# An explicit per-engine order for the first stage of an attention and two-MLP kernel, with block pairs merged to 512 columns

## The chip, the cores and the metric

The kernel runs on one core of a Trainium2 chip. The metric is the device time of one execution in microseconds (us); lower is better. TensorE is called PE, VectorE DVE, ScalarE ACT, GpSimd POOL, SyncE SP in the views. SP computes nothing here: it issues the DMA transfers, in the order of its queue.

## What is computed

Attention with a window of 64 positions over 4 batches of 576 positions and 8 heads of 64, then two gated MLPs, all on 2304 tokens:

```python
scores = scale * np.matmul(q, k.transpose(0, 1, 3, 2))
mask = (rel >= 0) & (rel < window)            # window = 64
scores = np.where(mask, scores, -1000000000.0)
...
attn = attn / (np.sum(attn, axis=-1, keepdims=True) + 1e-09)
x = np.matmul(attn, v)                        # to 2304 x 512
...
gate = 1.0 / (1.0 + np.exp(-(x @ w_gate)))    # 512 x 1536
x = gate * (x @ w_val) @ w_out                # 1536 x 512
...
return (x @ w_a) * (x @ w_b) @ w_out
```

q, k, v and x are float32; the weights come as 8-byte words that the kernel turns into float32 itself.

## The kernel before

**Blocks and tiles.** The 2304 tokens are nine blocks of 256 columns, each of two attention tiles of 128 tokens: 18 tiles. Blocks 0 to 4 (tiles 1 to 10, counted from 1 here and from 0 in the names) are the front; blocks 5 to 8 are the back, whose attention runs as filler beside the MLPs of the front.

**An attention tile** (`attention`, L103 to L197): load k, q and v; transpose k and q on PE into PSUM (kps, qps, L118); copy them out to kt and qt (L125, L126) and bring the last 64 columns of the tile before into kt (L123; a tile that starts a sequence is zeroed there, L121); 32 score products (sps, L138); add the mask and take the row's extreme on DVE (L148); exponentials on ACT, each with a read of its running sum (L153); add a constant to the sums and take the reciprocal on DVE (L169, L170); scale on POOL (L171); transpose back (tps, L178) and copy out to pt (L179); products with v (xps, L186), for which parts of v are moved between partitions by DMA (vb, L161 and L165); and split the result into a high part on ACT (xh, L192) and a low part on DVE (xl, L193).

**Weights.** A weight number F has three matrices a, b and o of 512 KB. `load_weights` loads them; `decode` (L274 to L307) turns each into a high and a low part: two operations on ACT (low and ex, L282, L285), two on DVE (wi, L287, L290), one on POOL (L293), then DVE (ex, L295), ACT (L300) and DVE (L301). It saves the pair (ka, kb, ko, 512 KB each, L303) and, for a and b, the float32 matrix (kf, 256 KB, L305) to DRAM for later. There are two buffers for ex, one for low and wi, three for raw words, four for each decoded matrix.

**Units.** One unit is one block (256 columns) or pair of blocks (512 columns) with one weight number: 12 products for the gate (gps), 12 for the value (vps, L317), then tanh on ACT, a product on DVE (hr, L341), and a split into hh (ACT, L326) and hl (DVE, L327). After the units of a turn follow the down projections (accm, L405; four pieces for a pair, two for a block), held back until the next turn, each evacuated to gacc by a copy on ACT for the first turn of a block and by an addition on DVE (L385) after that.

**Order.** `FIRST` lists the turns of the front's first stage. Before, these are block 0 with weights 0 and 1; block 1 with 0 to 2; block 0 with 2; then blocks 2, 3 and 4 with 0 to 2 each: 15 units of 256 columns. Behind it the turns go by the groups (0), (1, 2), (3, 4); the first is block 0 with weight 3. Within this the program gives a work list, and a scheduler of the framework chooses for each engine the order in which the instructions stand, by its own estimate of when each could run:

```python
    FIRST = (
        ((("attention", 0), ("weights", 0), ("weights", 1), ("attention", 1)), 0, (0, 1)),
        ((("weights", 2), ("attention", 2)), 1, (0, 1, 2)),
        ((), 0, (2,)),
        ((("attention", 3),), 2, (0, 1, 2)),
        ((("attention", 4),), 3, (0, 1, 2)),
        ((), 4, (0, 1, 2)),
    )
```

Of the kernel before, what the change touches and what calls it, by code (L numbers as in the profile page):

```python
# [9 lines left out]
F32 = mybir.dt.float32  # L10
# [10 lines left out]
def tile_window_attention_gated_mlps(ctx, tc, q, k, v, w1g, w1v, w1o, w2a, w2b, w2o, out):  # L21
# [4 lines left out]
    P = 128  # L26
# [37 lines left out]

    mask_n = qp.tile([P, P], F32, name="mask_n")
# [36 lines left out]

    def attention(t, dst, c0):  # L103
# [3 lines left out]
        mask = edge_mask(starts[0]) if starts else mask_n  # L107
        raw = [load_tile(nm, src, t, work, "kq", 3) for nm, src in (("k", k), ("q", q))]
        v_own = load_tile("v", v, t, vs, "v", 3)
        yield  # L110

# [3 lines left out]
        kqps = [kp.tile([P, NP, P], F32, tag=kq_tag, name=f"{nm}ps{t}") for nm in "kq"]  # L115
        for ps, r in zip(kqps, raw):
            for j in range(NP):
                nc.tensor.transpose(ps[:, j, :], r[:, 2 * j:2 * j + 2, :], ident)  # L118
        kt = kts.tile([P, NP, KW], F32, tag="kt", name=f"kt{t}")
        if starts == [0]:  # L120
            nc.vector.memset(kt[:, :, before], 0.0)  # L121
        else:
            nc.gpsimd.tensor_copy(kt[:, :, before], prev["k"][:, :, last])  # L123
        qt = qp.tile([P, NP, P], F32, tag="qt", bufs=2, name=f"qt{t}")
        nc.scalar.activation(out=kt[:, :, own], in_=kqps[0], func=AF.Copy)  # L125
        nc.scalar.activation(out=qt, in_=kqps[1], func=AF.Copy, scale=QSCALE)  # L126
        prev["k"] = kt
        yield
# [13 lines left out]
        yield  # L142
        stat = small.tile([P, 3, 2, NP], F32, tag="stat", name=f"stat{t}")
        ssum, nmax, den = (stat[:, i] for i in range(3))
        pr = [work.tile([P, NP, P], F32, tag="pr", bufs=4, name=f"pr{t}_{e}") for e in range(2)]
        for e in range(2):
            for j in range(NP):
# [3 lines left out]
                )  # L151
            for j in range(NP):
# [4 lines left out]
            yield  # L157
# [6 lines left out]
        else:  # L164
            nc.sync.dma_start(out=v_before[lo], in_=prev["v"][hi])  # L165
        prev["v"] = v_own
        pt = [work.tile([P, NP, P], F32, tag="pt", bufs=2, name=f"pt{t}_{e}") for e in range(2)]
        for e in range(2):
            nc.vector.tensor_scalar(out=den[:, e], in0=ssum[:, e], scalar1=1.0e-9, scalar2=None, op0=ALU.add)  # L169
            nc.vector.reciprocal(out=den[:, e], in_=den[:, e])  # L170
            nc.gpsimd.tensor_tensor(  # L171
                out=pr[e], in0=pr[e], in1=den[:, e].unsqueeze(2).to_broadcast([P, NP, P]), op=ALU.mult
            )
            yield
        for e in range(2):
# [3 lines left out]
            nc.scalar.activation(out=pt[e], in_=tps, func=AF.Copy)  # L179
            yield  # L180
        xps = ps_at.tile([P, NP, P], F32, tag="at", name=f"xps{t}")
        for j in range(NP):
            for s, vv in enumerate((v_before, v_own)):
                rows = slice(s * WIN, (s + 1) * WIN)
                for e, dims in enumerate((lo, hi)):
                    nc.tensor.matmul(  # L186
                        xps[dims, j, rows], lhsT=vv[:, 2 * j + e, :], rhs=pt[e][:, j, rows], start=True, stop=True
                    )
        cols = slice(c0, c0 + P)
        if isinstance(dst, tuple):  # L190
            xhi, xlo = (d[:, :, cols] for d in dst)
            nc.scalar.activation(out=xhi, in_=xps, func=AF.Copy)  # L192
            nc.vector.tensor_tensor(out=xlo, in0=xps, in1=xhi.bitcast(F32), op=ALU.subtract)  # L193
# [3 lines left out]
        yield  # L197
# [35 lines left out]
    def attention_stream(blocks):  # L233
# [3 lines left out]
        for tick in range(1 << 30):  # L237
# [4 lines left out]
            for blk, u in list(live):  # L242
                if next(u, u) is u:
# [6 lines left out]

    mats = ((w1g, w1v, w1o), (w2a, w2b, w2o))
    words = [[w.bitcast(I32) for w in m] for m in mats]
    staged, ready = {}, {}
# [6 lines left out]
    def load_weights(F):  # L260
        ph, fc = divmod(F, NF)
        sl = slice(2 * fc * P, 2 * (fc + 1) * P)
        for nm, w in zip("abo", words[ph]):
            r = stage.tile([P, DM, 2], I32, tag="st", name=f"st_{nm}")
            if nm == "o":
                nc.sync.dma_start(out=r.rearrange("p f t -> p (f t)"), in_=w[fc * P:(fc + 1) * P, :])
            else:
                nc.sync.dma_start(
                    out=r.rearrange("p (c f) t -> p c (f t)", c=NP),
                    in_=w[:, sl].rearrange("(c p) f -> p c f", p=P),  # L270
                )
# [534 lines left out]
```

## Time and profile before

| | |
|---|---|
| median of 3 runs | 987.81 us (986.78 to 989.71) |
| the profiled execution | 987.0 us, span 984.9 us |
| mean granted clock of PE | 0.985 |
| busy over the span | PE 954.0 us (97%), DVE 591.0 (60%), ACT 465.3 (47%), POOL 321.0 (33%) |
| chain of waits, share of the span | PE 80%, DVE 7%, DMA 6%, ACT 2%, issue 2%, POOL 2% |

The times were taken without the profiler; the profile is one more execution, and its span runs from the first to the last instruction. Shares over the span average over stages that have different limits; the rows further down are of single stretches. PE's busy time holds the modelled ends of pipelined products, so how fast PE really goes is read from the distance between starts.

### The profile page before, as it was taken

To read this page: it belongs to the slowest core of one execution; us is meant where nothing else is said; L and a number is where in the kernel's file an instruction comes from. 1 tells how busy PE (TensorE), PEld (TensorE's weight loads), DVE (VectorE), ACT (ScalarE), POOL (GpSimd) and SP (SyncE) were. 2 spreads that over 40 slices of the span, in tenths; PEclk is the share of its full clock that TensorE was granted. 3 is DMA by queue.
4 is the path that set the end of the run, shared out by engine and by line. 5 is a ranking of instruction groups with operands and counts; after the bars stand their busy time and mean duration, and the time that the engine had idled before them with its cause. 6 is when DMAs were issued, how large, how long until landed. Compare 5 with 4: busy or idle time off the path is not lost.

```text
span 984.9 us, 15767 instructions
## 1 busy us (share of the span) xinstructions
PE 954.0 (97%) x5774; PEld 809.1 (82%) x5774; DVE 591.0 (60%) x1175; ACT 465.3 (47%) x1059; POOL 321.0 (33%) x333
## 2 busy tenths in 40 slices
PE   5689999999999999999999999999999999999998
PEld 4579998798888887888888888888888878888886
DVE  4877467775675785466665273544564684455645
ACT  5978646655454665555543243452342444423221
POOL 4544213332221222121221243534430385434400
PEclk8699999999999999999999999999999999999999
DMA  9998268566666575455462245543334555442312
GB/s 257 316 300 254 64 185 294 152 227 190 186 187 184 166 230 152 160 171 184 150 206 103 86 150 193 192 144 127 132 134 150 190 179 185 150 147 89 107 43 85
DMA packets 122844, 167.48 MB, mean 170 GB/s; under 512 B 61840, under 2 KB 86416, under 8 KB 122768
## 3 DMA queue, kind: packets, MB, share of 16 engines
q1 hardware_dynamic: 122768, 166.49, 53.2%
q8 instruction: 45, 0.74, 0.3%
q14 instruction: 31, 0.25, 0.1%
HBM read 106.95 MB, written 55.05 MB: 164 GB/s over the span
## 4 chain that ended last, share of the span: by engine, by line
PE 80%; DVE 7%; DMA 6%; ACT 2%; issue 2%; POOL 2%; SPq 1%; DVEq 0%; POOLq 0%; ACTq 0%
PE gps L317 14%; PE vps L317 13%; PE qa L606 13%; PE accq L666 13%; PE acc L360 8%; PE qb L606 6%; PE accm L405 5%; PE qc L606 3%; DMA kf<-ex 3%; PE xps L186 1%; PE sps L138 1%; DMA k<-in_k_dram 1%; DVE ex L295 1%; PE tps L178 1%; POOL wi L293 1%
## 5 line engine op out<-in xcount | busy, mean ns | idle before, releaser
L293 POOL TENSOR_TENSOR wi<-wi,low 128x512 int32<-128x512 int32 x72 | 102.8, 1428 | 306.8 <-DVE wi L290 251.3
L317 PE MATMUL gps<-xh,wa 128*128 128x512 f32 (+1 forms) x624 | 174.0, 348 | 2.2 <-ACT xh L192 2.2
L317 PE MATMUL vps<-xh,wb 128*128 128x512 f32 (+1 forms) x624 | 171.4, 342 | 0.0
L317 PEld LDWEIGHTS gps<-xh,wa 128*128 128x128 f32 x624 | 111.6, 191 | 17.3 <-ACT xh L192 3.1
L591 POOL TENSOR_TENSOR wq<-s,wq 128x256 fp32r<-128x256 f32 x96 | 77.3, 810 | 147.6 <-ACT wq L590 147.4
L317 PEld LDWEIGHTS vps<-xh,wb 128*128 128x128 f32 x624 | 111.2, 190 | 13.8
L317 PE MATMUL gps<-xl,wa 128*128 128x512 f32 (+1 forms) x312 | 107.3, 344 | 0.0
L317 PE MATMUL vps<-xl,wb 128*128 128x512 f32 (+1 forms) x312 | 106.3, 341 | 0.0
L405 PE MATMUL accm<-hh,wo 128*128 128x256 f32 (+1 forms) x336 | 85.4, 331 | 1.3 <-DVE gacc L385 1.2
L670 DVE TENSOR_TENSOR res<-accq,res 128x512 f32<-128x512 f32 x80 | 54.3, 688 | 49.0 <-PE accq L666 48.8
L624 ACT ACTIVATE r<-qa 128x512 f32<-128x512 f32 x72 | 42.6, 594 | 83.3 <-PE qa L606 80.0
L295 DVE SCALAR_TENSOR_TENSOR ex<-ex,wi 128x512 f32<-128x512 f32 x72 | 53.0, 735 | 46.0 <-ACT ex L285 20.7
L606 PE MATMUL qa<-op,wq 128*128 128x512 f32 x288 | 75.5, 390 | 0.7 <-POOL op L548 0.7
L360 PE MATMUL acc<-wo,hh 128*128 128x512 f32 x240 | 74.7, 392 | 1.0 <-DVE res L670 0.8
L606 PE MATMUL qb<-op,wq 128*128 128x512 f32 x288 | 73.4, 389 | 0.0
L327 DVE SCALAR_TENSOR_TENSOR hl<-hr,hh 128x512 fp32r<-128x512 f32 (+1 forms) x78 | 53.3, 684 | 22.7 <-ACT hh L326 22.5
L326 ACT ACTIVATE hh<-hr 128x512 fp32r<-128x512 f32 (+1 forms) x78 | 41.2, 529 | 51.4 <-DVE hr L344 30.8
L317 PEld LDWEIGHTS vps<-xl,wb 128*128 128x128 f32 x312 | 59.2, 190 | 7.0
L317 PEld LDWEIGHTS gps<-xl,wa 128*128 128x128 f32 x312 | 59.6, 191 | 6.4 <-issue 0.2
L405 PEld LDWEIGHTS accm<-hh,wo 128*128 128x128 f32 x336 | 57.8, 190 | 8.0 <-DVE gacc L385 2.1
L588 POOL TENSOR_TENSOR s<-wf 128x256 f32<-128x256 f32 x48 | 39.5, 822 | 75.3 <-DMA wf<-kf 73.5
L606 PEld LDWEIGHTS qa<-op,wq 128*128 128x128 f32 x288 | 53.9, 188 | 12.2 <-POOL op L548 1.1
(123 smaller groups left out, 1954.9 us busy)
## 6 DMA issues: line engine op xcount, KB each, us to landing
wa<-ka SPq DMA_DIRECT2D x27, 512.0 KB, 3.2
wb<-kb SPq DMA_DIRECT2D x27, 512.0 KB, 3.3
wo<-ko SPq DMA_DIRECT2D x27, 512.0 KB, 4.6
st_o<-in_moe_w_out_dram SPq DMA_DIRECT2D x24, 512.0 KB, 4.5
kf<-ex SPq DMA_DIRECT2D x48, 256.0 KB, 4.3
ka<-wa SPq DMA_DIRECT2D x24, 512.0 KB, 3.0
kb<-wb SPq DMA_DIRECT2D x24, 512.0 KB, 3.5
ko<-wo SPq DMA_DIRECT2D x24, 512.0 KB, 3.0
```

The costliest lines, as they stand in the source:

```text
L293: nc.gpsimd.tensor_tensor(out=wi, in0=wi, in1=low, op=ALU.add)
L295: nc.vector.scalar_tensor_tensor(out=wf, in0=ex, scalar=SMALLEST, in1=wi.bitcast(F32), op0=ALU.is_ge, op1=ALU.mult)
L317: nc.tensor.matmul(ps, lhsT=a[:, c * P:(c + 1) * P], rhs=b[:, c, :], start=(n == 0), stop=(n == 3 * NP - 1))
L326: nc.scalar.activation(out=hh, in_=hr, func=AF.Copy, scale=factor)
L327: nc.vector.scalar_tensor_tensor(out=hl, in0=hr, scalar=factor, in1=hh.bitcast(F32), op0=ALU.mult, op1=ALU.subtract)
L360: nc.tensor.matmul(ps, lhsT=a[:, m * P:(m + 1) * P], rhs=b, start=begin and n == 0 and (phase == 1 or m % 2 == 0), stop=end and n == 2 and ...
L405: nc.tensor.matmul(ps[:, m], lhsT=a[:, sl], rhs=b, start=k == 0, stop=k == total - 1)
L591: nc.gpsimd.tensor_tensor(out=t[:, 1], in0=s, in1=t[:, 0].bitcast(F32), op=ALU.subtract)
L606: nc.tensor.matmul(ps, lhsT=a[:, c * P:(c + 1) * P], rhs=b[:, c, :], start=first and n == 0, stop=n == 5, skip_group_check=True,)
L624: nc.scalar.activation(out=r, in_=ps, func=AF.Copy)
L666: nc.tensor.matmul(ps, lhsT=a, rhs=b, start=n == 0, stop=n == len(pairs) - 1)
L670: nc.vector.tensor_tensor(out=dst, in0=ps, in1=dst, op=ALU.add)
```

## The change

The front's first stage is written as 454 steps. Each step puts the instructions of one engine (or one DMA) into the program, and a string, `RAMP`, gives the order: a to j are the ten tiles, L loads a weight matrix, D and W decode one, K saves one, P is one product group on PE, T one operation behind it. `in_order` then ties every instruction so far to the one ahead of it on its engine, without a semaphore, so the framework's scheduler cannot change this order; it may still place later instructions between.

- The turns are now (0), (1), (0), (2) with one weight each, (1, 2) with two, (0) with one, (3, 4) with three: five units of 256 columns and five of 512. The state after the stage is the same: weights 0 to 2 are done for all five blocks.
- `OTHERS` moves work of single tiles. On DVE in place of ACT: four copies to kt, four to qt, six to pt. For four tiles the exponentials keep no sum, and DVE sums each half (eight reductions, L199). One copy of a k tail goes from POOL to ACT.
- DVE's additions of down projections rise by six, since blocks 0, 1 and 2 come in more turns.
- The saves of decoded weights (K) stand late in the order.

```diff
-    FIRST = (
...
+    FIRST = (((0,),1),((1,),1),((0,),1),((2,),1),((1,2),2),((0,),1),((3,4),3))
+    STAGGERED, DECODED, BEHIND = False, 4, 0
+    RAMP = (
+        "a7b2La3cacb3a4Lbcb2a2dD2dbDbc2bacbc2bababDb2a2cLDW2cbc2W2eDead2Dbad2c2acd3b2DW2LDfcbcbcd3bDcdcW2De2f"
...
+    OTHERS = {
+        "k": (0, 2, 4, 8),
+        "q": (1, 4, 8, 9),
+        "sum": (2, 4, 6, 9),
+        "p": (0, 5, 7),
+        "norm": (),
+        "before": (0, 8, 9),
+    }
...
+    def moved(t, what, dst, src, scale=1.0):
+        if t in OTHERS[what]:
+            nc.vector.tensor_scalar(out=dst, in0=src, scalar1=scale, scalar2=None, op0=ALU.mult)
+        else:
+            nc.scalar.activation(out=dst, in_=src, func=AF.Copy, scale=scale)
...
-                    accum_out=None if False else ssum[:, e, j:j + 1],
+                    accum_out=None if t in OTHERS["sum"] else ssum[:, e, j:j + 1],
...
+            if t in OTHERS["sum"]:
+                nc.vector.tensor_reduce(out=ssum[:, e], in_=pr[e], op=ALU.add, axis=AX.X)
...
+    def in_order():
+        newest = {}
+        for i in nc.cur_bb.bb.instructions:
+            if i.engine in newest:
+                tc.add_manual_dep(
+                    i, newest[i.engine],
+                    mybir.DependencyInfo(mybir.DependencyClass.NoSync, mybir.DependencyReason.DATA), reason="in_order",
+                )
+            newest[i.engine] = i.name
...
+    streams = dict(zip("abcdefghijklmnopqr", tiles))
+    streams["L"] = call(lambda F=F, nm=nm: load_matrix(F, nm) for F, i, nm in order_of)
+    streams["D"] = (s for F, i, nm in order_of for s in decode_words(F, i, nm))
+    streams["W"] = (s for F, i, nm in order_of for s in decode_pair(F, i, nm))
+    streams["K"] = call(lambda F=F, nm=nm: save(F, nm, pairs.pop((F, nm))) for F, i, nm in order_of)
+    streams["P"] = call(iter(matmuls))
+    streams["T"] = (s for g in rest_of for s in g)
+    for what, count in re.findall(r"([A-Za-z])(\d*)", RAMP):
+        for _ in range(int(count or 1)):
+            next(streams[what])
+    in_order()
```

How the instructions now stand, at three places. First, SP's queue ahead of the loads of the fifth tile. In the names, st is a raw weight, kf, ka, kb, ko are stores of decoded ones; the fifth tile's k is k_562, in two pieces because it crosses a batch boundary. Before:

```order
L268 DMA st_a<-in_moe_w_gate_dram 128x4x256
L305 DMA kf_140<-ex 128x512
L268 DMA st_b<-in_moe_w_val_dram 128x4x256
L100 DMA k_459<-in_k_dram 128x8x64
L303 DMA ka_137<-wa 128x1024
L100 DMA q_461<-in_q_dram 128x8x64
L305 DMA kf_140<-ex 128x512
L303 DMA kb_138<-wb 128x1024
L266 DMA st_o<-in_moe_w_out_dram 128x1024
L100 DMA k_562<-in_k_dram 64x8x64 x2
```

Now (the fifth tile's k is k_469):

```order
L315 DMA st_b<-in_moe_w_val_dram 128x4x256
L109 DMA v_327<-in_v_dram 128x8x64
L109 DMA k_339<-in_k_dram 128x8x64
L109 DMA q_345<-in_q_dram 128x8x64
L191 DMA vb_408<-v_301 64x512
L195 DMA vb_408<-v_243 64x512
L313 DMA st_o<-in_moe_w_out_dram 128x1024
L367 DMA kf_140<-ex 128x512
L109 DMA k_469<-in_k_dram 64x8x64 x2
```

The three loads of the second weight, the second kf, ka and kb of the first weight no longer stand ahead of it.

Second, PE behind the last xps of the tenth tile. Before, the products that follow belong to a unit of block 3 (xl_3, xh_3) of 256 columns that is already under way:

```order
L186 MATMUL xps_1810<-pt_0_1771,v_1537 64x64
L186 MATMUL xps_1810<-pt_1_1772,v_1537 64x64
L317 MATMUL vps<-xl_3_833,wb 128x256
L317 MATMUL vps<-xh_3_832,wb 128x256
L317 MATMUL gps<-xh_3_832,wa 128x256
L317 MATMUL gps<-xl_3_833,wa 128x256
```

Now:

```order
L221 MATMUL xps_1716<-pt_0_1675,v_1394 64x64
L221 MATMUL xps_1716<-pt_1_1714,v_1394 64x64
L489 MATMUL accm<-hh,wo 128x512
L489 MATMUL accm<-hl,wo 128x512
L489 MATMUL accm<-hh,wo 128x512 x2
L489 MATMUL accm<-hl,wo 128x512
L489 MATMUL accm<-hh,wo 128x512
L136 MATMUL qps_2085<-ident,q_2060 128x128 x4
L389 MATMUL gps<-xh_3_237,wa 128x512
```

The first units of blocks 3 and 4 moved behind the tenth tile, with one piece of the down projection of blocks 1 and 2 between.

Third, DVE in the middle of the stage, where the copies and sums now stand between the steps of the decode. Now:

```order
L411 SCALAR_TENSOR_TENSOR hr<-hr,vps 128x256
L114 TENSOR_SCALAR pt_0_1070<-tps_0_1029 128x512
L341 TENSOR_SCALAR wi<-st_o 128x512
L344 SCALAR_TENSOR_TENSOR wi<-st_o,wi 128x512
L400 SCALAR_TENSOR_TENSOR hl<-hr,hh 128x256
L230 TENSOR_TENSOR xl_1_236<-xps_995,xh_1_235 128x4x128
L199 TENSOR_REDUCE stat_989<-pr_0_990 128x4
L200 TENSOR_SCALAR stat_989<-stat_989 128x4
L201 RECIPROCAL stat_989<-stat_989 128x4
L114 TENSOR_SCALAR pt_1_1116<-tps_1_1107 128x512
```

The two L114 rows were on ACT before, and the L199 row is new.

## Rows read from the trace of the kernel before

**Rows 1.** Busy us by stretch: stretch, length, PE, PEld, DVE, ACT, POOL, PEclk, DMA, GB/s.
```profile
20.00:100.00 80.00, 64.39 (x745) 57.71 (x738) 61.51 (x212) 64.66 (x199) 37.96 (x33) 0.87 0.98 289
8.50:127.50 119.00, 97.61 (x1147) 87.95 (x1140) 81.46 (x294) 89.65 (x277) 49.04 (x44) 0.89 0.84 239
150.00:178.40 28.40, 28.40 (x167) 23.68 (x165) 23.86 (x51) 19.95 (x46) 10.07 (x8) 1.00 0.79 261
```

**Rows 2.** Chain of waits of the first 200 us: start, us, what.
```profile
25.78 5.17 DMA k<-in_k_dram
...
95.55 0.66 PE qps L118 x4
```

**Rows 3.** DMA view: the first 86 us, then one issue row of the span.
```profile
DMA packets 36744, 24.85 MB, mean 289 GB/s; under 512 B 27575, under 2 KB 32701, under 8 KB 36733
...
ka<-wa SPq DMA_DIRECT2D x24, 512.0 KB, 3.0
```

**Rows 4.** SP's queue in order of time: the tenth tile's k.
```profile
86.03 0.39 SPq L100 DMA_DIRECT2D k<-in_k_dram  x1
```

**Rows 5.** PE in order of time, 127 to 151 us: start, us, group.
```profile
127.31 0.39 PE L317 MATMUL vps<-xl,wb 128*128 128x256 f32 x1
...
143.48 0.28 PE L317 MATMUL gps<-xh,wa 128*128 128x256 f32 x1
...
146.36 0.28 PE L405 MATMUL accm<-hh,wo 128*128 128x256 f32 x1
...
150.68 0.40 PE L317 MATMUL gps<-xh,wa 128*128 128x512 f32 x1
```

**Rows 6.** PE in order of time, 171 to 180 us.
```profile
171.12 0.62 PE L405 MATMUL accm<-hh,wo 128*128 128x512 f32 x2
171.57 0.39 PE L405 MATMUL accm<-hl,wo 128*128 128x512 f32 x1
...
179.93 0.49 PE L405 MATMUL accm<-hh,wo 128*128 128x512 f32 x1 [1.17 <-DVE gacc L385]
```

**Rows 7.** DVE in order of time, 41 to 46 us.
```profile
41.53 0.28 DVE L148 CUSTOM_DVE_ANT_0 pr<-sps,mask_n 128x128 f32<-128x128 f32 x1
...
41.74 0.28 DVE L148 CUSTOM_DVE_ANT_0 pr<-sps,mask_n 128x128 f32<-128x128 f32 x1
...
43.61 0.42 DVE L287 TENSOR_SCALAR wi<-st_a 128x512 int32<-128x512 int32 x1
43.95 0.16 DVE L169 TENSOR_SCALAR stat<-stat 128x4 f32<-128x4 f32 x1
44.02 0.68 DVE L301 TENSOR_TENSOR wo<-ex,wo 128x512 fp32r<-128x512 f32 x1
44.62 0.68 DVE L290 SCALAR_TENSOR_TENSOR wi<-st_a,wi 128x512 int32<-128x512 int32 x1
45.22 0.17 DVE L170 RECIPROCAL stat<-stat 128x4 f32<-128x4 f32 x1
...
45.59 0.18 DVE L170 RECIPROCAL stat<-stat 128x4 f32<-128x4 f32 x1
```

**Rows 8.** Groups by line on DVE, 8.5 to 127.5 us: busy, mean ns, idle before.
```profile
L295 DVE SCALAR_TENSOR_TENSOR ex<-ex,wi 128x512 f32<-128x512 f32 x14 | 12.2, 870 | 8.8 <-POOL wi L293 4.2 <-issue 2.8 <-POOL kt L123 1.6
...
L341 DVE SCALAR_TENSOR_TENSOR hr<-hr,vps 128x256 f32<-128x256 f32 x10 | 4.2, 416 | 6.1 <-PE vps L317 6.1
L301 DVE TENSOR_TENSOR wb<-ex,wb 128x512 fp32r<-128x512 f32 x4 | 3.6, 891 | 0.6 <-ACT wb L300 0.6
```

**Rows 9.** ACT in order of time, 42 to 47 us.
```profile
41.95 0.19 ACT L153 ACTIVATION_READ_ACCUMULATOR pr<-pr,stat 128x1 f32 x1
42.05 0.39 ACT L153 ACTIVATE pr<-pr,stat 128x128 f32<-128x128 f32 x1
...
46.30 0.58 ACT L179 ACTIVATE pt<-tps 128x512 f32<-128x512 f32 x1
46.78 0.58 ACT L125 ACTIVATE kt<-kps 128x512 f32<-128x512 f32 x1
```

More of the change, by code (lines that the diff above doesn't have):

```diff
@@ L1 @@
+import re
 from contextlib import ExitStack
@@ L122, in attention @@
         else:
-            nc.gpsimd.tensor_copy(kt[:, :, before], prev["k"][:, :, last])
+            copy = (lambda *a: nc.scalar.activation(*a, AF.Copy)) if t in OTHERS["before"] else nc.gpsimd.tensor_copy
+            copy(kt[:, :, before], prev["k", t - 1][:, :, last])
+        yield
+        ps = transposed("q", q_own)
+        yield
         qt = qp.tile([P, NP, P], F32, tag="qt", bufs=2, name=f"qt{t}")
[L125 to L128, printed above, removed]
+        moved(t, "q", qt, ps, QSCALE)
+        yield True
         sp, s_tag = (ps_gv, "gv") if t < 2 else (ps_at, "at")
@@ L141, in attention @@
                     )
[L142 to L145, printed above, removed]
+        yield True
+        pr = []
         for e in range(2):
+            if e == 0:
+                stat = small.tile([P, 3, 2, NP], F32, tag="stat", name=f"stat{t}")
+                ssum, nmax, den = (stat[:, i] for i in range(3))
+                mask = edge_mask(starts[0]) if starts else mask_n
+            pr.append(work.tile([P, NP, P], F32, tag="pr", bufs=4, name=f"pr{t}_{e}"))
             for j in range(NP):
@@ L242, in attention_stream @@
             for blk, u in list(live):
-                if next(u, u) is u:
+                step = next(u, u)
+                while step is None:
+                    step = next(u, u)
+                if step is u:
                     live.remove((blk, u))
@@ L248, in attention_stream, with whole @@
                 yield
+    def whole(steps):
+        while True:
+            try:
+                next(steps)
+            except StopIteration as end:
+                return end.value
     mats = ((w1g, w1v, w1o), (w2a, w2b, w2o))
     words = [[w.bitcast(I32) for w in m] for m in mats]
-    staged, ready = {}, {}
+    staged, parts, ready = {}, {}, {}
     kept = {
@@ new lines, in load_weights, with save, decode_words @@
+    def load_weights(F):
+        for nm in "abo":
+            if (F, nm) not in staged and nm not in parts.get(F, {}):
+                load_matrix(F, nm)
+    def save(F, nm, pair):
+        nc.sync.dma_start(out=kept[F, nm], in_=pair.bitcast(F32))
+    wordy = {}
+    def decode_words(F, i, nm):
+        st = staged.pop((F, nm))
+        w0, w1 = st[:, :, 0], st[:, :, 1]
+        low = dec.tile([P, DM], I32, tag="low", name="low")
+        nc.scalar.activation(out=low, in_=w0.bitcast(U32), func=AF.Copy, scale=2.0 ** -29)
+        yield
+        ex = dec.tile([P, DM], F32, tag="ex", bufs=2, name="ex")
+        nc.scalar.activation(out=ex, in_=w1.bitcast(F32), func=AF.Abs)
+        yield
+        wi = dec.tile([P, DM], I32, tag="wi", name="wi")
+        nc.vector.tensor_scalar(
+            out=wi, in0=w1, scalar1=3, scalar2=(1 << 30) - 1, op0=ALU.logical_shift_left, op1=ALU.bitwise_and
+        )
+        nc.vector.scalar_tensor_tensor(
+            out=wi, in0=w1, scalar=-(1 << 30), in1=wi, op0=ALU.bitwise_and, op1=ALU.bitwise_or
+        )
+        yield
+        nc.gpsimd.tensor_tensor(out=wi, in0=wi, in1=low, op=ALU.add)
+        wordy[F, nm] = ex, wi
+        yield
@@ L307, in decode @@
-        ready[F] = got
+            if nm not in parts.get(F, {}):
+                whole(decode_words(F, i, nm))
+                whole(decode_pair(F, i, nm))
+                save(F, nm, pairs.pop((F, nm)))
+                yield
+        ready[F] = parts[F]
     def product(ps, w, x):
@@ L463, in turns @@
         if ph == 0:
-            for _, b, fcs in FIRST:
-                take((b,), len(fcs))
-        for j, g in enumerate(order):
-            take(g, 1 + j * (G - 1) // (len(order) - 1))
+            for g, n in FIRST:
+                take(g, n)
+        if ph or not STAGGERED:
+            for j, g in enumerate(order):
+                take(g, 1 + j * (G - 1) // (len(order) - 1))
         for _ in range(NF // G):
```

242 lines of the change are left out of this document (148 added, 94 removed).

## The prediction

> **What bounds the kernel now.** I read the busy times by stretch first, because one mean over the span mixes two different programs. Over the span TensorE is busy 97%, and from the slice at about 100 us on its digit is 9. Only the front differs: from 20 to 100 us PE is busy 64.39 of 80 us at a mean granted clock of 0.87, while the DMA share is 0.98 [rows 1]. So whatever this change wins, it wins ahead of 100 us, and it counts only if PE later has no new gap.
>
> The second view is the chain of waits. In the front it hops between the engines and the DMA queue, with loads of k among its longest pieces (5.17 us at 25.78); from 95.55 us it stays on PE while the stage is finished [rows 2]. The DMA view of the first 86 us says why: 24.85 MB at 289 GB/s with the engines counted as full, and 27575 of 36744 packets below 512 bytes [rows 3]. The load of k for the tenth tile is issued at 86.03 us [rows 4]. The front is therefore paced by what stands ahead of each tile's load on SP's queue, with VectorE (61.51 of 80 us) and ScalarE (64.66) at about four fifths behind it [rows 1].
>
> The third view is PE in order of time. The last attention product of tile 10 (xps) ends its turn at 127.31 us. From there PE runs without a gap to the first unit after the stage, block 0 with weight 3, at 143.48; that unit's two products last to 146.36, and the held-back down projection of block 4 lasts to 150.68 [rows 5]. If that unit's 2.88 us are taken out, the stage's work is done at 150.68 − 2.88 = 147.8 us. That is the mark I compare with. The next gap on PE is at 179.93 us, 1.17 us, ended by VectorE adding a down projection [rows 6].
>
> **The change, part by part.**
>
> *PE's work.* Ten units of 256 columns become five of 512. Each unit has 24 up and 12 down products, so 360 instructions become 180. The 24 products of a 256-column unit take 2.88 us (143.48 to 146.36), or 0.12 each; two of 512 columns take 0.45 (171.12 to 171.57), or 0.227 each [rows 5, 6]. 360 × 0.12 = 43.2 against 180 × 0.227 = 40.9: 2.3 us less. The rows give 13 ns per product over the array's own time (0.120 against 256 / 2.4 = 107 ns, and 0.227 against 213). By the Trainium skill ("TensorE: Matmul & The Clock Gate", Back-to-back issue gap) that excess is 2.5 ns per product at the full clock, so by it the same merge would be worth 0.45 us; no row here shows so small an excess, and the sum goes by the rows.
>
> *What has to wait.* Blocks 3 and 4 share an operand, so none of their units can start before tile 10 is through. Before, block 3 needed tiles 7 and 8 alone, and its units ran while tiles 9 and 10 were in attention. Call T the time at which PE has finished xps of tile 10. Behind T now stand: 6 down products of blocks 1 and 2 (1.36 us), 72 up products of 512 columns (16.34), 12 down products of block 0 (1.44) and 36 of blocks 3 and 4 (8.17), in all 27.3 us. Before, it was 147.8 − 127.3 = 20.5. So the mark moves to T + 27.3, and **the change gains only if T is below 147.8 − 27.3 = 120.5 us**. It was 127.3.
>
> *DMA.* In the order of before, 25.6 MB are requested ahead of k of tile 10: twelve 512 KB saves of decoded weights and sixteen weight loads of the same size among them [rows 3]. Now it is 15.9 MB, with three saves and eight loads. At 289 GB/s that is 55 us in place of the 86.03 measured [rows 3, 4]. The saves stand behind tile 10 and are not read in the front. On SP's queue tile 5's k moves ahead of three weight loads and three stores. So DMA stops setting T. The loads still wait for buffers, so a late transpose on PE holds what stands behind it on SP.
>
> *ScalarE.* Fourteen copies out of PSUM leave it (0.48 us each, 46.30 to 46.78 [rows 9]), and 32 exponentials lose their accumulator read, after which the next starts 0.10 us later (41.95 to 42.05) [rows 9]: 6.7 + 3.2 = 9.9 us less, of 89.65 busy between 8.5 and 127.5 us [rows 1]. It was the busier of the two, and falls below VectorE. One copy of a k tail moves from GpSimd to it; tiles 1 and 10 start a sequence and zero that part instead. That one costs less than the 0.48 us of a whole copy.
>
> *VectorE.* It takes the fourteen copies and eight sums. No such copy from PSUM is in the trace. Lower end: a one-source operation on SBUF starts the next after 0.34 us (43.61 to 43.95). Upper end: 512 columns with two sources, 0.60 us (44.02 to 44.62) [rows 7]. I take 0.60 for both, since the additions of PSUM are the nearest. At 0.34 the fourteen would cost 3.6 us less. By the Trainium skill ("VectorE: DVE Perf Modes", The perf-mode tier table) single-source fp32 work from PSUM does not get the doubled rate, which speaks against the cheap end; no row here shows it.
>
> I now count VectorE's work until T by the distance from start to start. On both sides: 80 scores × 0.21 (41.53 to 41.74), 20 pairs of a small addition and a reciprocal × 0.37 (45.22 to 45.59) [rows 7], nine xl (the tenth comes behind T) × 0.60, 29.6 us. Weights: now the first two operations (0.34 + 0.60) ten times, the third ten and the fourth nine times at 0.60: 20.8. Before, up to 127.5 us, 15, 14 and 12 times: 29.7 (14 is the row of L295; L301 has three operands of four each) [rows 8]. Units: a 256-column operation lasts 416 ns where one of 512 lasts 680 and starts the next after 600, so I take 0.34; now five units of 256 (2 × 0.34) and two of 512 (2 × 0.60): 5.8; before ten of 256: 6.8 [rows 7, 8]. Additions of down projections: now 4 × 0.60 = 2.4, before 1.2. New copies and sums: 22 × 0.60 = 13.2. That is 71.8 now and 67.3 before. Measured before: 81.46 us busy [rows 1], 1.21 times the count; some operations run longer than these rows (L295 lasts 870 ns in the mean). Now that gives 71.8 × 1.21 = 87 us, which must fit between the first scores (8.5 us) and T.
>
> *How full can VectorE be?* At 100% T = 8.5 + 87 = 95.5. At its share of 20 to 100 us, 61.51 / 80 = 77%, T = 121.5. From 150 to 178.4 us it reached 23.86 / 28.4 = 84% in a free order [rows 1]. With DMA out of the way I take 90%, between 84% and 100%: **T = 105**.
>
> *After the stage.* The mark is then 105 + 27.3 = 132.3, a gain of 15.5. Not all arrives: from 150 to 178.4 us VectorE is busy 23.86 of 28.4 us and ends PE's next gap [rows 1, 6]; with PE there 15 us earlier and 16 us more done on VectorE, its slack of 4.5 us goes. I take back 2.5 (ends: nothing, and 5). Beyond, PE is the bound and its instructions are the same, so the gain reaches the end.
>
> Sum: 15.5 − 2.5 = 13 us. The profiled execution took 987.0 us (span 984.9); 974. The median of the three runs shown is 987.81, so against it the forecast is **975 us**.
>
> **The rivals.**
>
> *Slower: the pairing starves PE.* The place is the last two tiles: no unit of blocks 3 and 4 is left to run beside them. If an order fixed per engine keeps VectorE at 77% or less (each engine's next step waits for one that could have been passed), T is 121.5 or later. At 121.5 the mark comes 1 us late, and with the 2.5 the time is 991; at the old T of 127.3 it is 6.8 + 2.5 later, 997. The switch is T = 120.5. For it: VectorE gets more work, and SP's loads stand behind stores that wait for VectorE. Against: PE still has 12 us of units of blocks 0 to 2 placed between tile 10's scores and its xps, and the DMA queue is short.
>
> *Full packing.* VectorE is kept at 97 to 100%, T is 95 to 98 and nothing is given back: 987.8 − 24 = 964. For: ScalarE and DMA no longer bind. Against: tile 10's chain is some ten dependent steps on four engines, and 77 to 84% is what the rows show with a free order.
>
> *No real change.* VectorE reaches 80 to 83%, T is 113 to 117, the gain of 3 to 7 is eaten later: 986. That is also what comes out if the new order is not what sets T: were the loads or PE the limit at the old places, the tied order would only re-sort idle time.
>
> **How the numbers follow.** Forecast (970 to 982) 0.55, full packing 0.15, no real change 0.13, slower 0.17. A measurement of this kernel tells 0.3%, 3 us, from no change. Faster: 0.55 + 0.15 + a third of the third case, 0.74. Within: 0.10. Slower: 0.16. The range: full packing's 964 less a little for a cheap copy, and up to where T is 120.5: 963 to 990; it leaves out the worse part of the slower case (0.1) and some luck below.
>
> **What would show it.** Right: SP issues tile 10's k near 55 to 60 us; xps of tile 10 ends on PE near 105; VectorE is busy about 90% from 20 to 100 us and ScalarE less than it; block 0 with weight 3 starts near 126 to 130; past 200 us the stretches look as before. Wrong: DMA still at 0.98 up to 100 us (the loads are held by buffers, not by the queue); VectorE at 77% with long waits for PE or ScalarE; PE gaps in the units after T; or a gap on PE between 135 and 180 us larger than the stage won. If the copies on VectorE take 0.34, the total comes out some 4 us lower.

## Result and profile after

The changed kernel takes 965.6 us (median of 4 runs, 964.8 to 966.9); the kernel before, run beside it, 987.6. The ratio is 0.9775 with a 95% interval of 0.9757 to 0.9794: 22 us less, where 13 were forecast (975). The profiled execution took 965.8 us with a span of 964.0, so spans differ by 20.9.

In this part and below, T is the start of PE's first instruction behind the last xps of tile 10, as in the prediction: 127.31 before [rows 5]. PE in order of time, after (a bracket is the idle time ahead of a row and what ended it):

```profile
42.78 1.10 PE L164 MATMUL sps<-kt,qt 64*64 64x128 f32 x32 [0.16 <-ACT qt L116]
...
97.17 0.33 PE L221 MATMUL xps<-pt,v 128*64 128x64 f32 x3
97.43 0.50 PE L489 MATMUL accm<-hh,wo 128*128 128x512 f32 x1
...
118.57 0.28 PE L389 MATMUL gps<-xh,wa 128*128 128x256 f32 x1
...
121.44 0.40 PE L489 MATMUL accm<-hh,wo 128*128 128x512 f32 x1
...
179.68 0.50 PE L489 MATMUL accm<-hh,wo 128*128 128x512 f32 x1 [1.27 <-DVE gacc L467]
```

T is 97.43. Block 0's unit with weight 3 runs from 118.57 to 121.44, and the 36 down products of blocks 3 and 4 (8.17 us) stand behind it, so the mark of the prediction is 121.44 − 2.88 + 8.17 = 126.7 against 147.8: 21.1 us earlier, and the end is 20.9 earlier. Nothing was given back in between. The row to look at longest is the first: between 42.78 and 179.68 us no row has a bracket.

The stretches show where T came from. Before, not shown ahead of the prediction:

```profile
8.50:43.00 34.50, 18.86 (x216) 14.89 (x208) 27.15 (x97) 26.75 (x84) 17.55 (x15) 0.68 1.12 315
43.00:127.30 84.30, 78.55 (x934) 72.87 (x930) 54.30 (x200) 62.81 (x193) 31.49 (x29) 0.97 0.73 208
```

After, the same columns (stretch, length, PE, PEld, DVE, ACT, POOL, PEclk, DMA, GB/s); the last two rows answer to [rows 1]:

```profile
8.50:43.00 34.50, 26.24 (x360) 22.53 (x364) 30.68 (x125) 29.12 (x93) 17.90 (x19) 0.85 1.00 236
43.00:97.40 54.40, 54.40 (x642) 48.78 (x634) 46.62 (x163) 43.14 (x122) 21.16 (x21) 1.00 0.96 275
...
20.00:100.00 80.00, 75.62 (x913) 67.16 (x910) 69.84 (x252) 65.25 (x181) 32.65 (x33) 0.97 0.96 264
...
8.50:97.40 88.90, 80.64 (x994) 71.31 (x994) 77.30 (x288) 72.25 (x214) 39.05 (x39) 0.94 0.98 260
```

From 8.5 us to T PE's idle time falls from 15.6 + 5.8 = 21.4 us to 8.3, 13.1 less. Its busy time falls from 97.41 (18.86 + 78.55) to 80.64, 16.8 less; 6.8 of that is work that moved behind T (27.3 − 20.5), at most 2.3 the merge, and some 8 us remain. Part of them is work that now runs at 2.4 GHz in place of 1.2: the granted clock ahead of 43 us is 0.85 in place of 0.68, and by an estimate from these rows (busy time times the missing share of the clock, 18.86 × 0.32 + 78.55 × 0.03 before against 26.24 × 0.15 now) that is some 4.5 us. Where the other 3 or so lie is not shown. 13.1 + 16.8 is the 29.9 us by which T moved. Behind T stand 6.8 us more, so 23.1 should arrive and 21.1 did; of the 2 us between, 1.3 are products of tile 11's attention (qps at 98.93, sps at 104.95 and 115.14), which before stood behind the mark.

SP's queue, after: the tenth tile's k, to set beside [rows 4].

```profile
65.83 0.96 SPq L109 DMA_DIRECT2D k<-in_k_dram  x1
```

VectorE's groups by line, 8.5 to 97.4 us (busy, mean ns, idle before), to set beside [rows 8]:

```profile
L354 DVE SCALAR_TENSOR_TENSOR ex<-ex,wi 128x512 f32<-128x512 f32 x10 | 7.4, 740 | 0.0
...
L200 DVE TENSOR_SCALAR stat<-stat 128x4 f32<-128x4 f32 x20 | 5.7, 284 | 2.3 <-ACT pr L183 2.1
L199 DVE TENSOR_REDUCE stat<-pr 128x4 f32<-128x512 f32 x8 | 5.4, 674 | 0.0
...
L114 DVE TENSOR_SCALAR pt<-tps 128x512 f32<-128x512 f32 x6 | 4.0, 672 | 0.9 <-PE tps L211 0.9
...
L114 DVE TENSOR_SCALAR qt<-qps 128x512 f32<-128x512 f32 x4 | 2.7, 679 | 1.5 <-PE qps L136 1.5
```

The copies out of PSUM last 672 to 679 ns and the sums 674, as long as the two-source operation (0.68 us, 0.60 from start to start [rows 7]) that is the upper of the two prices of the prediction.

### The profile page after: what moved, and what is told of

Same layout as the page of the kernel before. It is cut to its first block, busy times and chain, and to the rows that moved or that the text cites. A ratio compares the mean times of both kernels' runs of the same rounds, so it can differ in the third digit from the quotient of the medians.

```text
span 964.0 us, 15333 instructions
## 1 busy us (share of the span) xinstructions
PE 945.2 (98%) x5594; PEld 794.5 (82%) x5594; DVE 597.9 (62%) x1193; ACT 454.4 (47%) x1004; POOL 320.1 (33%) x332
## 4 chain that ended last, share of the span: by engine, by line
PE 73%; DVE 4%; DMA 2%; POOL 1%; issue 1%; ACT 1%; SPq 0%; DVEq 0%; POOLq 0%; ACTq 0%
PE qa L708 13%; PE accq L768 12%; PE gps L389 12%; PE vps L389 12%; PE acc L442 8%; PE qb L708 6%; PE accm L489 3%; PE qc L708 3%; DMA kf<-ex 1%; PE xps L221 1%; PE sps L164 1%; DMA wf<-kf 1%; DVE op L650 1%; PE tps L211 1%; DVE gacc L467 1%
## 5 line engine op out<-in xcount | busy, mean ns | idle before, releaser
L389 PE MATMUL gps<-xh,wa 128*128 128x512 f32 (+1 forms) x584 | 169.9, 358 | 0.3 <-DVE hr L411 0.3
L389 PE MATMUL vps<-xh,wb 128*128 128x512 f32 (+1 forms) x584 | 166.8, 352 | 0.0
L389 PEld LDWEIGHTS gps<-xh,wa 128*128 128x128 f32 x584 | 104.9, 189 | 16.6 <-DVE hr L411 0.5
L389 PEld LDWEIGHTS vps<-xh,wb 128*128 128x128 f32 x584 | 105.0, 189 | 15.3 <-issue 0.2
L389 PE MATMUL gps<-xl,wa 128*128 128x512 f32 (+1 forms) x292 | 102.8, 352 | 0.0
L489 PE MATMUL accm<-hh,wo 128*128 128x512 f32 (+1 forms) x296 | 85.0, 355 | 1.4 <-DVE gacc L467 1.3
L354 DVE SCALAR_TENSOR_TENSOR ex<-ex,wi 128x512 f32<-128x512 f32 x72 | 51.1, 710 | 40.9 <-ACT ex L338 19.5
L708 PEld LDWEIGHTS qb<-op,wq 128*128 128x128 f32 x288 | 54.1, 188 | 11.2
L489 PEld LDWEIGHTS accm<-hh,wo 128*128 128x128 f32 x296 | 53.0, 189 | 9.7 <-DVE gacc L467 1.8
L389 PEld LDWEIGHTS gps<-xl,wa 128*128 128x128 f32 x292 | 55.2, 189 | 6.9
L400 DVE SCALAR_TENSOR_TENSOR hl<-hr,hh 128x512 fp32r<-128x512 f32 (+1 forms) x73 | 49.1, 672 | 18.4 <-ACT hh L398 18.2
```

The source lines that it names most:

```text
L354: nc.vector.scalar_tensor_tensor(out=wf, in0=wf, scalar=SMALLEST, in1=wi.bitcast(F32), op0=ALU.is_ge, op1=ALU.mult)
L389: nc.tensor.matmul(ps, lhsT=a[:, c * P:(c + 1) * P], rhs=b[:, c, :], start=(n == 0), stop=(n == 3 * NP - 1))
L400: nc.vector.scalar_tensor_tensor(out=hl, in0=hr, scalar=factor, in1=hh.bitcast(F32), op0=ALU.mult, op1=ALU.subtract)
L489: nc.tensor.matmul(ps[:, m], lhsT=a[:, sl], rhs=b, start=k == 0, stop=k == total - 1)
L708: nc.tensor.matmul(ps, lhsT=a[:, c * P:(c + 1) * P], rhs=b[:, c, :], start=first and n == 0, stop=n == 5, skip_group_check=True,)
```

## Experiments

Two theories were set against each other. **Theory VectorE** is the forecast's: T is VectorE's work divided by how full it can be kept. **Theory PE** was formed from the rows above: from 43 us on PE is full, so its own work sets the end, and the gain is the idle and half-clock time that vanished ahead of it. Differences in time are from the ratios, (ratio − 0.9775) × 987.6; the interval of a ratio is about ± 0.0017, 1.7 us. "Moved T" is against 97.43.

| kernel | median us | ratio (95%) | time against the changed kernel | T | moved T |
|---|---|---|---|---|---|
| e1_free | 993.2 | 1.0057 (1.0042 to 1.0073) | +27.9 | 129.23 | +31.8 |
| e9_sp | 987.8 | 1.0009 (0.9993 to 1.0024) | +23.1 | 123.94 | +26.5 |
| e10_notsp | 975.8 | 0.9886 (0.9869 to 0.9902) | +11.0 | 109.48 | +12.1 |
| e4_pairs | 1005.5 | 1.0175 (1.0156 to 1.0195) | +39.5 | 144.01 | +46.6 |
| e3_split | 968.6 | 0.9808 (0.9793 to 0.9823) | +3.3 | 98.78 | +1.4 |
| e5_saves | 968.8 | 0.9812 (0.9797 to 0.9828) | +3.7 | 101.05 | +3.6 |
| e2_act | 967.9 | 0.9805 (0.9786 to 0.9824) | +3.0 | 100.17 | +2.7 |
| e6_dve | 969.8 | 0.9817 (0.9801 to 0.9833) | +4.1 | 101.57 | +4.1 |
| e7_pe | 972.0 | 0.9845 (0.9828 to 0.9861) | +6.9 | 103.28 | +5.9 |
| e8_warm | 965.8 | 0.9778 (0.9763 to 0.9793) | +0.3 | 98.87 | +1.4 |
| e11_noadd | 965.3 | 0.9783 (0.9766 to 0.9801) | +0.8 | 97.17 | −0.3 |
| e12_less | 965.5 | 0.9777 (0.9759 to 0.9794) | +0.2 | 98.01 | +0.6 |

Where T moves by a few us, the time moves by about as much: T is the right thing to watch. Where it moves by 26 to 47 us, 3 to 7 of them are made up behind it.

### The order taken away: e1_free, e9_sp, e10_notsp

```diff
-    in_order()                                    # e1_free
-            if i.engine in newest:
+            if i.engine in newest and i.engine == nc.sync.engine:    # e9_sp
+            if i.engine in newest and i.engine != nc.sync.engine:    # e10_notsp
```

> The same 454 steps, but the tie per engine is taken away, so the framework's scheduler may reorder within the stage; it puts weight loads and decode steps earlier. If the gain of 22 us comes from the merge and the moved work alone, the time stays within 3 us of the changed kernel's 965.6. If the order itself carries it, the kernel falls back to 975 to 988, with k of tile 10 issued later than 66 us and PE's idle time and half-clock stretches back ahead of 45 us. The forecast's theory (VectorE is the bound) says the same number through another path: T (97.4 us in the changed kernel) moves to 105 to 118.

> Only SP's queue stays tied to the written order; the scheduler orders PE, VectorE, ScalarE and GpSimd as it likes. With the tie gone from all engines the time was 993.2. If the place of the loads ahead of the weights and saves is what the order brings (q of tile 2 no longer 7.8 us late), most of the 28 us comes back: 966 to 973. If the order on the computing engines carries it, the time stays at 985 to 994. Theory PE says the split by PE's idle time and half-clock time ahead of 43 us.

> The reverse: the four computing engines stay tied to the written order, SP's queue is free, and the scheduler puts three weight loads ahead of q of tile 2. Those are 1.6 MB at some 240 to 300 GB/s, 5 to 6 us that every later step of a tied order waits for. If the loads' place decides, 985 or more, with one wait of 5 to 8 us on PE ahead of 20 us; if the computing engines' order decides, 966 to 972.

Without the tie the same steps take 993.2 us, more than the 975 to 988 that I expected: in a free order the merge and the moved work lose 6 us against the kernel before, and **the written order is worth all of the gain and more**. With SP's queue alone tied, 23.1 of the 27.9 us stay lost; with the other four engines tied, 11.0. So the computing engines' order is the larger part and SP's the smaller, and they overlap (23.1 + 11.0 is more than 27.9). My expectation for e10_notsp split on this and named the wrong total: it gives 975.8, between its two cases. The wait it named is there. PE in order of time, e10_notsp:

```profile
16.58 1.09 PE L136 MATMUL qps<-ident,q 128*128 128x128 f32 x4 [8.32 <-DMA q<-in_q_dram]
```

The free queue puts three raw weights ahead of q of tile 2, and every later step of the tied engines waits these 8.3 us; another 3.08 us on a q follow at 55.93. With SP alone tied the loads are in time and PE waits for computing steps instead. Waits of PE in e9_sp, 5 to 97 us (total, times, longest):

```profile
PE sps L164 <- ACT qt L116: 5.3, 3, 3.3
PE kps L136 <- ACT kt L116: 5.1, 1, 5.1
...
```

Its DMA share from 20 to 100 us is 0.73 while PE is busy 65.99 of 80 us: there the DMA queue is plainly not the bound, and the time is still that of the kernel before.

### The merge alone: e4_pairs

```diff
...
-        ((("attention", 3),), 2, (0, 1, 2)),
-        ((("attention", 4),), 3, (0, 1, 2)),
-        ((), 4, (0, 1, 2)),
...
+        ((("weights", 2),), (1, 2), (1, 2)),
+        ((), (0,), (2,)),
+        ((("attention", 3), ("attention", 4)), (3, 4), (0, 1, 2)),
```

> The kernel before with the turns merged as in the change and nothing else: no written order, no tie, no work moved between engines, saves where the scheduler puts them. If merging alone gave the gain, 966. By the price of the products alone, 2.3 us: 985. By the rival of the forecast (no unit of blocks 3 and 4 left to run beside the last tiles, T no earlier than before), 991 to 997.

1005.5 us: the merge in a free order costs 18 us against the kernel before, more than the rival's 991 to 997. PE runs out of units, as the rival says, but more of it shows at another place. PE in order of time, e4_pairs:

```profile
70.00 0.58 PE L317 MATMUL gps<-xh,wa 128*128 128x256 f32 x1 [3.56 <-ACT xh L192]
...
98.33 0.56 PE L317 MATMUL gps<-xh,wa 128*128 128x256 f32 x1 [3.32 <-ACT xh L192]
...
137.94 0.33 PE L186 MATMUL xps<-pt,vb 128*64 128x64 f32 x2 [1.99 <-ACT pt L179]
```

In the first two rows PE stands before the units of blocks 1 and 2, whose operand a tile has not yet delivered; such waits sum to 8.3 us, where the kernel before has 2.2. The rival named the last two tiles. They are in the third row, and the stretch is:

```profile
130.80:144.00 13.20, 10.25 (x154) 8.30 (x153) 5.09 (x26) 7.40 (x24) 2.60 (x4) 0.82 0.60 136
```

No unit is left to run beside them, and PE idles 3 us there at a granted clock of 0.82. T is 144.01, later than before, which the rival had put at 127.3.

### The price of a product: e3_split

```diff
+                halves = [slice(0, N), slice(N, W)] if split else [slice(None)]
+                for i, h in enumerate(halves):
...
+                        ps[:, h], lhsT=a[:, c * P:(c + 1) * P], rhs=b[:, c, h],
```

> Every product of 512 columns in the stage is issued as two of 256 in the same place of the order: 180 more instructions, nothing else. By the rows' 13 ns each this costs 2.3 us, so 968; by the smaller price of 2.5 ns it costs 0.45, so 966. Theory PE (from 43 us on PE's own work sets the end): the whole price arrives at the end. Theory VectorE: the part of it ahead of T (about a third) is hidden, 1.5 us arrive. T itself moves by 0.5 to 1 us under PE, not at all under VectorE.

+3.3 us, within about 2.4 (two intervals of 1.7 combined). The rows' price of 13 ns (2.3 us) is inside that, and 0.45 us just outside. PE in order of time, e3_split, a split product of weights a:

```profile
109.62 0.40 PE L391 MATMUL gps<-xl,wa 128*128 128x256 f32 x2
109.86 0.64 PE L391 MATMUL gps<-xh,wa 128*128 128x256 f32 x4
110.34 0.40 PE L391 MATMUL gps<-xl,wa 128*128 128x256 f32 x2
```

Four take 0.48 us, 0.12 each, against 0.227 for one of 512. The Trainium skill ("TensorE: Matmul & The Clock Gate", Back-to-back issue gap) has 2.5 ns at the full clock, for the isolated gap of one product; these float32 products show 13.

### Saves early: e5_saves

```diff
-...cbc2W2eDead2Dbad2c2acd3b2DW2LDfcbcbcd3bDcdcW2De2f
...
+...cbc2W2KeDead2Dbad2c2acd3b2DW2LDfcbcbcd3bDcdcW2KDe2f
...
```

> The changed kernel, but each save of a decoded matrix stands right behind its decode: 1, 2, 3, 4 and 6 saves ahead of the loads of tiles 6, 7, 8, 9 and 10 in place of 0, 0, 0, 0 and 3. Three saves of 524 KB at some 260 GB/s are 6 us of transfer. If the place of the loads on SP's queue still sets T, tile 10's k is issued near 72 us, T is 4 to 8 us later and the time 969 to 974. If PE's work sets it and the loads have slack (tile 10's transpose began 8.6 us after k's issue), k is issued later but T and the time stay within 2 us: 965 to 968.

k of tile 10 is issued at 70.30 us, T is 3.6 us later and the time 3.7. It lies between the two cases. PE waits 1.00 us for ACT's copy of q at 60.96 and 0.79 us for VectorE at 63.76, where the changed kernel has no gap. Late saves are worth some 4 of the 22 us (± 2.4).

### More and less work on VectorE: e6_dve, e2_act, e11_noadd

```diff
+        if t < 10:                                                     # e6_dve
+            nc.vector.tensor_reduce(out=junk, in_=qt, op=ALU.add, axis=AX.X)
-        "k": (0, 2, 4, 8),                                             # e2_act: all lists empty
+        "k": (),
...
-            nc.vector.tensor_scalar(out=den[:, e], in0=ssum[:, e], ...)  # e11_noadd
-            nc.vector.reciprocal(out=den[:, e], in_=den[:, e])
+            nc.vector.reciprocal(out=den[:, e], in_=ssum[:, e])
```

> Ten unused row sums (512 columns, 0.67 us each) are added on VectorE, one in each front tile behind its copy of q: 6.7 us more VectorE work ahead of T, nothing on other engines. Theory VectorE: T and the end move by 6 to 7 us, 972. Theory PE: VectorE is idle 11.6 of the 88.9 us from 8.5 to T and takes most of it there; only the sums of the tiles ahead of 43 us (six) stand on the path, so 0 to 3 us arrive, 966 to 969.

> The changed order with the table of moved work empty: 14 copies from PSUM and the sums of 4 tiles are back on ScalarE, one k tail back on GpSimd's copy. VectorE loses 22 x 0.67 = 15 us of work ahead of T, ScalarE gains 6.7 us of copies and about 3 us of accumulator reads. Theory VectorE: T comes earlier or stays, 958 to 966. Theory PE (PE alone sets the end from 43 us on, the order fitting round it): ScalarE, busy 72 of 89 us ahead of T, rises to 82 of 89, and steps placed where ScalarE now is late make PE wait; 968 to 975, the more of it ahead of 45 us the less it can be made up.

> The changed kernel without the addition of 1e-9 to the softmax sums (the row's extreme is taken off first, so a sum is at least 1 and float32 holds the same number with or without it). VectorE loses 20 operations of 0.28 us ahead of T (5.7 us busy, some 3.8 by start to start), each on a tile's chain from exponential to scaling. Ten sums of 0.67 us added in each tile cost 4.1 us. Theory VectorE: T and the end come 4 to 6 us earlier, 960 to 962. Theory PE: only what shortens the waits ahead of 43 us arrives (five tiles, two additions each), 0 to 2 us: 963.5 to 965.5.

6.7 us more on VectorE move the end by 4.1 us, less than theory VectorE's 6 to 7 and just above theory PE's 3; with ± 2.4 it excludes neither. Work given back to ScalarE (VectorE is then busy 65.73 us of the 88.9 in place of 77.30, 11.6 less where 15 were counted) costs 3.0: ScalarE is then the busiest (79.97 us). The clear one is e11_noadd, where VectorE loses work and no one gains any:

```profile
43.00:97.40 54.40, 54.40 (x635) 48.75 (x628) 43.88 (x153) 42.93 (x123) 20.49 (x21) 1.00 0.95 273
...
8.50:97.40 88.90, 80.71 (x995) 71.58 (x996) 71.72 (x270) 72.37 (x216) 39.35 (x39) 0.94 0.99 259
```

VectorE is busy 71.72 us in place of 77.30, and T moves by 0.3, the time not at all. **Theory VectorE falls.** PE is full from 43 us on with or without those 5.6 us.

### More and less work on PE: e7_pe, e12_less

```diff
-        product(ps[nm], w[nm], x)
+        for _ in range(times):                       # e7_pe: 2 for (block 0, weight 1), (block 2, weight 0)
+            product(ps[nm], w[nm], x)
...
+        terms = ((wh, xh), (wh, xl), (wl, xh))[:1 if short else 3]    # e12_less: the same two units
```

> The up products of block 0 with weight 1 and of block 2 with weight 0 are issued twice (48 products of 256 columns at 0.12 us): 5.8 us more PE work between 50 and 80 us, nothing else changes. Theory PE: all of it arrives, T and the end move by 5.8 us, 971. Theory VectorE: PE has room ahead of T, so T stays within 2 us and the end moves by 0 to 2, 966 to 968.

> The up products of block 0 with weight 1 and block 2 with weight 0 keep only the high part times the high part: 32 products of 256 columns (0.12 us) are left out between 50 and 75 us, 3.8 us of PE work; the low-part terms of these two units are missing from the output. The other direction of doubling them (which cost 5 to 7 us). Theory PE: all of it arrives, T near 93.6, 961.8. If another engine stands close behind PE (VectorE is busy 86% of 43 to 97.4 us), less arrives: T 95 to 97, 963.5 to 965.5, and PE has gaps after 50 us. Theory VectorE: nothing, 965 to 966.

Adding 5.8 us moves T by 5.9 and the end by 6.9 (interval ± 2.4): theory PE's 5.8 lies within that, and theory VectorE's 0 to 2 is out. Taking 3.8 us away moves nothing, and there theory PE fails. e12_less, the stretch, and three of PE's gaps in it:

```profile
43.00:97.40 54.40, 51.29 (x602) 44.61 (x599) 47.27 (x165) 42.94 (x123) 21.03 (x21) 1.00 0.96 276
```

```profile
55.95 0.63 PE L211 MATMUL tps<-ident,pr 128*128 128x128 f32 x4 [0.89 <-ACT kt L116]
56.92 0.39 PE L490 MATMUL accm<-hh,wo 128*128 128x256 f32 x1 [0.35 <-ACT gacc L466]
...
81.00 1.10 PE L164 MATMUL sps<-kt,qt 64*64 64x128 f32 x32 [0.77 <-DVE qt L114]
```

PE has 3.1 us of gaps, nearly all that was taken out; by what ended them, 1.9 of it waits for ScalarE and 1.2 for VectorE. The chain of waits of e12_less around the last of them (start, us, what):

```profile
72.57 0.60 DVE ex L354
73.16 0.09 DVE stat L200
73.25 0.04 SPq L367
73.30 0.05 issue
73.35 5.73 DMA st_o<-in_moe_w_out_dram
...
79.10 0.44 DVE wi L341
...
79.56 0.69 DVE wi L344
80.25 0.61 DVE qt L114
```

On SP's queue the load of a raw weight (st_o) stands behind a store (kf, L367) that waits for VectorE's ex. The load takes 5.73 us; VectorE's next step is its decode, and tile 10's copy of q stands behind that; PE waits for the copy. In the changed kernel that load is issued at 73.17 us, 0.2 earlier, and is there by 78.15, so most of what e12_less loses here is the transfer itself (5.73 us against at most 4.98); why it took longer is not shown. In the changed kernel the same places read, on VectorE and ScalarE:

```profile
78.15 0.61 DVE L341 TENSOR_SCALAR wi<-st_o 128x512 int32<-128x512 int32 x1
...
79.40 0.68 DVE L114 TENSOR_SCALAR qt<-qps 128x512 f32<-128x512 f32 x1
```

```profile
78.21 0.69 ACT L335 ACTIVATE low<-st_o 128x512 int32<-128x512 uint32 x1 [1.88 <-DMA st_o<-in_moe_w_out_dram]
```

ScalarE waited for that load until 78.21, VectorE came to it at 78.15 without a gap, and PE began the scores at 80.44, 0.4 us after the copy of q (79.40 + 0.68) was done. Three paths meet within half a microsecond there.

### A warmer PE: e8_warm

```diff
+        if t in (1, 2, 3, 4):
+            for j in range(NP):
+                nc.tensor.matmul(sps[0][:, j, :], lhsT=ident, rhs=ident, start=True, stop=True)
```

> Four unused 128x128 products of the identity stand ahead of the scores of tiles 2 to 5, where PE waits for the copies of q (0.89 to 2.35 us of gap each) and its clock is granted at 0.66 to 0.84 of full. If the work of PE in these gaps raises the granted clock between 15 and 30 us, up to 3 us of half-speed work is saved: 963. If the clock stays as it is, they cost 0 to 1 us: 966 to 967. VectorE theory: no effect either way, since T is set elsewhere.

No change. The granted clock did rise, and fell later. e8_warm, five stretches:

```profile
10.00:15.00 5.00, 3.89 (x56) 3.35 (x56) 3.59 (x14) 3.71 (x14) 3.19 (x4) 1.00 1.17 237
15.00:20.00 5.00, 2.45 (x48) 1.80 (x48) 4.16 (x20) 3.92 (x18) 2.79 (x3) 1.00 1.05 231
20.00:25.00 5.00, 3.40 (x50) 2.93 (x45) 4.97 (x22) 4.17 (x12) 1.76 (x3) 1.00 0.80 238
25.00:30.00 5.00, 3.30 (x66) 2.91 (x68) 4.86 (x25) 4.63 (x15) 2.90 (x3) 0.75 1.03 239
30.00:35.00 5.00, 5.00 (x33) 4.88 (x31) 4.50 (x10) 3.77 (x12) 1.61 (x2) 0.57 0.90 232
```

The same stretches of the changed kernel:

```profile
10.00:15.00 5.00, 4.13 (x46) 3.74 (x47) 3.87 (x15) 3.71 (x16) 3.73 (x4) 0.68 1.21 242
15.00:20.00 5.00, 2.86 (x52) 2.16 (x52) 4.16 (x16) 3.38 (x15) 2.79 (x4) 0.84 1.09 226
20.00:25.00 5.00, 3.03 (x34) 2.68 (x30) 4.93 (x23) 4.72 (x13) 1.76 (x2) 0.80 0.88 258
25.00:30.00 5.00, 4.38 (x67) 3.52 (x68) 4.35 (x24) 3.50 (x10) 2.36 (x3) 0.66 1.08 248
30.00:35.00 5.00, 4.42 (x60) 3.95 (x58) 4.82 (x10) 4.75 (x18) 1.62 (x2) 1.00 0.80 198
```

With the clock at 1.0 or 0.5 of full (2.4 or 1.2 GHz), these shares give some 10 us at half the clock in the changed kernel and some 7 in e8_warm (twice the missing share, times 5 us). So part of the half-clock time went; the rest moved from PE's waiting stretches to a later one, the end of it with PE full, and T came 1.4 us later. Weighted by how busy PE is in each stretch, the estimate of PE's time lost to the clock falls only from 3.9 to 3.0 us.

## Why the prediction was right and wrong

**Sign and place: right; the times named: too late.** All of the gain lies ahead of 100 us, PE has no new gap behind it, and from the mark on nothing is lost. The switch (gain only if T is below 120.5) holds in the runs: e9_sp with T at 123.94 and e1_free with 129.23 are no better than before, e10_notsp with 109.48 gains 11. T came at 97.43 where 105 was forecast, and block 0 with weight 3 at 118.57 where 126 to 130 were.

**What paces the kernel before: half right.** I read SP's queue as the pacemaker. The queue alone put in order brings 5 us of the 28 that the order is worth (e9_sp against e1_free), the computing engines' order alone 17 (e10_notsp against e1_free). The waits of e9_sp show the rest: steps of ScalarE and VectorE that a free order puts too late.

**The merge's price** (2.3 us by the rows, against 0.45 by the figure of the Trainium skill) holds by the rows, in e3_split. What I did not price is that the merge needs the order: in a free one it costs 18 us (e4_pairs).

**DMA: size nearly right, sign read wrong.** k of tile 10 is issued at 65.83 us, where 55 to 60 were forecast and 86.03 stood before. I named a DMA share of 0.98 up to 100 us as a sign against the forecast. It is 0.96 from 20 to 100 us, and yet PE does not wait for a load after 43 us: the share says that transfers are under way, not that anyone needs them. e12_less shows how near they are all the same.

**VectorE's work: mis-sized.** I scaled a count of 71.8 us by 1.21, what the kernel before showed over its own count, to 87. VectorE was busy 77.30 us from 8.5 to T, 1.08 times the count. The copies and sums came at the upper price as taken; the Trainium skill's rule that single-source float32 work from PSUM does not get the doubled rate ("VectorE: DVE Perf Modes", The perf-mode tier table) agrees with these 672 to 679 ns. What did not carry over from the old order is how long other operations last (740 ns in the mean at L354, where L295 had 870 [rows 8]). The trace of before shows which are the long ones, on VectorE and, behind the dots, on GpSimd:

```profile
46.76 1.51 DVE L295 SCALAR_TENSOR_TENSOR ex<-ex,wi 128x512 f32<-128x512 f32 x1 [0.20 <-POOL wi L293]
52.03 0.69 DVE L295 SCALAR_TENSOR_TENSOR ex<-ex,wi 128x512 f32<-128x512 f32 x1 [0.85 <-POOL wi L293]
...
46.68 2.49 POOL L171 TENSOR_TENSOR pr<-pr,stat 128x512 f32<-128x512 f32 x2
50.40 1.60 POOL L293 TENSOR_TENSOR wi<-wi,low 128x512 int32<-128x512 int32 x1 [0.69 <-DVE wi L290]
```

The first runs beside an operation on GpSimd, the second begins when one has ended (50.40 + 1.60). Of the fourteen L295, the five of 0.81 to 1.51 us all run beside GpSimd, and the other nine take 0.66 to 0.69. The same holds for every VectorE operation of the stretch that lasts over 12% longer than the median of its line without GpSimd beside it: 20 of them before, 10.6 us over the medians in sum, and 14 now, 4.8 us. That is 5.8 of the 9.7 us by which 87 was too much. That GpSimd is the cause was not tested by a run of its own.

**The share of 90%: the step that failed.** It came out as 77.30 / 88.9 = 87%, but the prediction's equation, T as VectorE's work over the share at which it is kept busy, is not what sets T: 5.6 us less VectorE work moved T by 0.3 (e11_noadd). With 1.08 the equation gives T = 8.5 + 71.8 × 1.08 / 0.9 = 94.7, and 964 in all; that this is close to 965.6, and that the measured time fell into the stated range, is luck as far as this step goes. PE, named as waiting, is full from 43 us on, and adding to PE costs all of what is added (e7_pe). Nor is PE the bound alone (e12_less). What shows in its place is a balance: more work on VectorE or PE costs some 60% of itself or more (4.1 for 6.7 us and 6.9 for 5.8, each ± 2.4), as a later load does; less work on one of them wins nothing. That the written order brings PE, VectorE with ScalarE, and the loads to the same places at the same time was followed at one place, the copy of q of tile 10 near 80 us, and is argued for the others.

**After the stage** I took back 2.5 us; nothing was. PE's next gap is 1.27 us where it was 1.17 [rows 6], although VectorE has more to do.

**The rivals.** The time is that of full packing (964, T 95 to 98, nothing given back), but by less work on VectorE, 87% full, not by 97 to 100%. The slower rival did not occur in the changed kernel; in e4_pairs T is later than it said, with most of the added waits ahead of the place that it named.

Still open: less work on PE and on VectorE at once, with that load of a raw weight earlier on SP's queue, was not tried. Nor was a written order without the merge: what the order would give with units of 256 columns, and the merge within a written order beyond the price of its products, is not shown. None of these kernels is measurably faster than the changed one.

## What to carry to other kernels

Where several engines share one long stage, price the order before the work: the same steps in a scheduler's order were 28 us slower than in a written one, and the merge that looked like a small gain was a loss without it. To find the bound of such a stage, add work to one engine at a time and also take some away; this stage, in balance, charged for the first and paid nothing for the second, and the first test alone would have named PE as the bound. A share of busy time near 1, of the DMA engines above all, is not a wait.

## What was not expected of the hardware

Unused products ahead of 25 us raised the granted clock there from 0.68 to 0.84 up to 1.00; between 30 and 35 us, with PE full, it was then 0.57 where it had been 1.00. PE had been busy 5.85 of the 10 us (15 to 25 us) before it fell. Some 3 of 10 us at half the clock went away, and the time did not change. And the same operation on VectorE (L295) lasted 0.66 to 0.69 us in nine cases and 0.81 to 1.51 in five, and all of these five ran beside an operation on GpSimd.
